# Routed attention with a gated feed-forward: another order of the first microseconds and of the last branch

## The chip, the core and the metric

The kernel runs on one NeuronCore of a Trainium2 chip. A core has five engines, each with its own queue of instructions: TensorE (PE, matrix products; the loading of its stationary operand is shown as PEld), VectorE (DVE), ScalarE (ACT), GpSimd (POOL) and SyncE (SP), which here only issues transfers. Engines wait for each other through semaphores. Products land in PSUM, all else lies in SBUF; transfers between HBM and SBUF go through 16 DMA engines. The metric is the time of one execution on the device in microseconds (us); smaller is better.

## What is computed

The reference has two blocks. The first is attention in which a query sees only keys of its own cluster; the second is a feed-forward with a hard swish. B, H, S, D = 4, 8, 768, 64; there are 16 centroids for each head; the second block has d_model 512 and d_ff 2048. All is float32.

```python
# q, k, v: (4, 8, 768, 64); centroids: (8, 16, 64)
q_assign = argmax(einsum('bhsd,hcd->bhsc', unit(q), unit(centroids)))
k_assign = argmax(einsum('bhsd,hcd->bhsc', unit(k), unit(centroids)))
mask   = q_assign[:, :, :, None] == k_assign[:, :, None, :]
scores = where(mask, (q @ k^T) / 8, -1e9)
attn   = softmax(scores) @ v
x = attn as (4*768, 512)
h = x @ w_in                      # (3072, 2048)
g = h * clip(h + 3, 0, 6) / 6
out = g @ w_out                   # (3072, 512)
```

## The kernel before

**Two paths.** `fast_path` computes the result on the assumption that the data are well-behaved (no ties between clusters, weights in a usual range, no row that sees almost nothing) and keeps sums from which this is read off at the end. It leaves one flag, `ok`. The kernel then loads `ok` into a register of each engine and, under `tc.If(... == 0)` in line 992, runs `general_path`, which computes everything again without the assumption. With the inputs of the reference `ok` is 1 and the general path is skipped, but its instructions stand in the program of each engine all the same: on SyncE 260 of them lie between the branch and what follows the `If`.

**Tiling.** The 32 heads are worked off as 16 pairs (two heads of 64 columns fill the 128 rows of TensorE). For a pair, `load` (line 175) brings q and k in four transfers and v in two. `turn` (line 287) transposes q and k by TensorE, three 128x128 blocks at a time into a PSUM tile `pqk`, and ScalarE copies each tile to `xf`: parts 0 and 1 are q, parts 2 and 3 are k. `cluster_scores` (line 303) multiplies `xf` by the unit centroids `cnT` into `pcs`, and ScalarE copies it to `cs`. `route` (line 314) transposes that back (`pr`), VectorE takes the maximum and writes `one_hot`. `route_turn` (line 343) multiplies `one_hot` by `ident_q` or `ident_k` (the identity, and the identity times -2^60, both bf16) into `po`, and ScalarE copies it to `xm`. Scores are then two products into one PSUM tile `ps`: `scores_qk` (line 361) from `xf`, which needs no routing, and a masked product from `xm`, which adds a huge negative number wherever the clusters differ. ScalarE takes the exponential, GpSimd adds up the rows for the sums, TensorE multiplies by v.

**The loop and what lies beside it.** One loop of 196 half-steps goes over all pairs (12 score tiles each). Beside the scores it works off the next pair's preparation, the decoding of the weights (they arrive as 64-bit numbers) and the products of the feed-forward of the batch before. The order of all engines' instructions is the order in which the program writes them: the whole of this stands under `tc.manual_schedule()`, and no planner moves anything. An engine works its own queue strictly in this order, so an instruction that waits holds up all that stand behind it.

**The prologue** (lines 588 to 603) is what the loop needs for its first pair. In order: the centroids are requested on ScalarE's queue, q and k of pair 0 on SyncE's, then `constants` (line 256: the identity, its two bf16 copies on VectorE, `parity`, and five fills on GpSimd), v and the first piece of the weights, `centroid_norm` (line 271: a chain of small VectorE operations that makes the centroids' rows unit length, spreads them to the two halves, transposes them by TensorE into `pc` and copies that to `cnT`), the four turns, the request for pair 1, two tiles of score products, the cluster scores, the routing. Small PSUM tiles of the prologue (`pqk`, `pc`, `pcs`, `pr`, `po`) come from `psum_m`, which has two buffers; a third tile waits until the first is read. `psum_t`, with one buffer, is used by the decoding of weights. There is one `qk` tile, so pair 1 can be requested only when pair 0 has been turned.

**The end.** After the last product of the feed-forward VectorE reduces the sums to `ok` (lines 646 to 665), each engine loads it, compares, and branches. After the `If` the kernel ends in two barriers over all engines. In the empty arm of the `If` each engine waits for its own semaphores (SyncE for eight).

Of the kernel before, what the change touches and what calls it, by code (L numbers as in the profile page):

```python
# [8 lines left out]
F32 = mybir.dt.float32  # L9
# [9 lines left out]
P = 128  # L19
# [21 lines left out]
FAR = 2.0**60  # L41
# [75 lines left out]
def fast_path(ctx, tc, ok, q, k, v, centroids, moe_w_in, moe_w_out, out):  # L117
# [3 lines left out]
    nc = tc.nc  # L121
# [21 lines left out]
    psum_t = pool("psum_t", 1, space=PSUM)  # L143
# [5 lines left out]
    ident = const.tile([P, P], F32, name="ident")  # L149
    ident_q = const.tile([P, P], BF16, name="ident_q")  # L150
    ident_k = const.tile([P, P], BF16, name="ident_k")
# [12 lines left out]
    st = {}  # L164
    later = []

    def scratch(shape, name):

        if st["early"]:
            return psum_m.tile(shape, F32, name=name, tag="m")  # L170
        return psum_t.tile(shape, F32, name=name, tag="t")
# [3 lines left out]
    def load(g, *names):  # L175
        if g >= NPAIR:
            return
        b, h = divmod(2 * g, H)
        for name in names:
            if name == "v":  # L180
                dst = st["v", g] = vp.tile([P, NCH, 2, D], F32, name="vt")
            elif name == "q":
                st["qk", g] = qkp.tile([P, 2, NCH, 2, D], F32, name="qk")
            if name != "v":
                dst = st["qk", g][:, "qk".index(name)]
            src = {"q": q, "k": k, "v": v}[name]
            for t in range(2):
                nc.sync.dma_start(dst[:, :, t], src[b, h + t].rearrange("(p j) d -> p j d", p=P))
# [66 lines left out]

    def constants():
        make_identity(nc, ident)
        nc.vector.tensor_copy(out=ident_q, in_=ident)
        nc.vector.tensor_scalar_mul(out=ident_k, in0=ident, scalar1=-FAR)
        for t in range(2):  # L260
            nc.vector.tensor_reduce(
                out=parity[:, t : t + 1],
                in_=ident.rearrange("p (h t c) -> p t h c", t=2, c=C)[:, t], axis=AX.XY, op=ALU.max,
            )
        nc.gpsimd.memset(half_c, 0.5)
        nc.gpsimd.memset(low_c, 1.0 / BOUND)
        nc.gpsimd.memset(ones, 1.0)
        nc.gpsimd.memset(w_low, W_LOW)
        nc.gpsimd.memset(one_hot, 0.0)

    def centroid_norm():
        cn = unit_rows(nc, smallp, cen, D)

        nc.scalar.activation(out=w_totals[:, 0, 0:1], in_=w_low, func=ACT.Exp)

        wide = smallp.tile([P, 2, D], F32, name="cenwide")
        for t in range(2):
            nc.vector.tensor_scalar_mul(out=wide[:, t], in0=cn, scalar1=parity[:, t : t + 1])
        pc = scratch([P, P], "pc")
        nc.tensor.transpose(out=pc, in_=wide, identity=ident)  # L280
        nc.vector.tensor_copy(out=cnT, in_=pc)


# [3 lines left out]
    def turn(g, part):  # L287
        if part == 0:
            st["xf", g] = xp.tile([P, NC2, P], F32, name="xf")
        qk, xf = st["qk", g], st["xf", g]  # L290
        pt = scratch([P, NHC, P], "pqk")
        for i in range(NHC):
            j = part * NHC + i
            nc.tensor.transpose(out=pt[:, i], in_=qk[:, j // NCH, j % NCH], identity=ident)  # L294
        dst = xf[:, part * NHC : (part + 1) * NHC]
        nc.scalar.copy(out=dst, in_=pt)  # L296
        if part == 3:
            st.pop(("qk", g))
# [4 lines left out]
    def cluster_scores(g):  # L303
        c0, xf = (2 * g) % H * C, st["xf", g]
        ps = scratch([P, 512], "pcs")[:, 0 : NC2 // 4 * P]
        for a in range(4):
            nc.tensor.matmul(  # L307
                ps[a * 2 * C : (a + 1) * 2 * C], lhsT=cnT[:, c0 : c0 + 2 * C], rhs=xf[:, a::4],
                start=True, stop=True,
            )  # L310
        cs = st["cs", g] = rtp.tile([P, NC2 // 4, P], F32, name="cs")
        nc.scalar.copy(out=cs, in_=ps)

    def route(g):
        cs = st.pop(("cs", g))
        pr = scratch([P, NC2, 2, C], "pr")
        for i in range(NC2 // 4):
            nc.tensor.transpose(out=pr[:, 4 * i : 4 * i + 4], in_=cs[:, i], identity=ident)
        pr = pr.rearrange("p j t c -> p (j t) c")
        mx = rtp.tile([P, 2 * NC2], F32, name="mx")  # L320
        nc.vector.reduce_max(out=mx, in_=pr, axis=AX.X)
        oh = one_hot.rearrange("p j (t c) -> p j t c", t=2)[:, :, :, 0:C]
        pr = pr.rearrange("p (j t) c -> p j t c", t=2)
        mx = mx.rearrange("p (j t) -> p j t", t=2)
        halves = [slice(0, NCH), slice(NCH, NC2)]
        for sl, op in zip(halves, (ALU.is_ge, ALU.is_lt)):
            nc.vector.tensor_tensor(
                out=oh[:, sl], in0=pr[:, sl],
                in1=mx[:, sl].unsqueeze(3).to_broadcast([P, NCH, 2, C]), op=op,
            )  # L330


        def count():
            for a, sl in enumerate(halves):
                seen = rtp.tile([P, NCH, 2, C], BF16, name="seen")
                nc.scalar.activation(
                    out=seen, in_=oh[:, sl], func=ACT.Copy, scale=1.0 - 2 * a,
                    accum_out=counts[:, a, g : g + 1],
                )

        later.append(count)
# [19 lines left out]
    def scores_qk(n):  # L361
        g, hf, j = where(n)
        st["ps", n] = psum_s.tile([P, 2, 512], F32, name="ps")
        scores_part(n, st["xf", g], True)
# [223 lines left out]
    with tc.manual_schedule():  # L588
        nc.scalar.dma_start(cen, centroids.rearrange("h c d -> (h c) d"))
        load(0, "q", "k")  # L590
        constants()
        load(0, "v")
        load_weights(0)
        centroid_norm()
        for part in range(4):
            turn(0, part)
        load(1, "q", "k")
        scores_qk(0)
        scores_qk(1)
        cluster_scores(0)  # L600
        route(0)
        for part in range(3):
            route_turn(0, part)

        for n in range(0, total + lag_d + 2, 2):
            g, r = divmod(n, per_pair)
            for i in (n, n + 1):
                if i < total:
                    scores(i)
            for i in (n - lag_v, n - lag_v + 1):  # L610
                if 0 <= i < total:
                    attn_v(i)
            m = n - lag_d + 1
            if m >= 0 and m % NCH == NCH - 1:
                later.append(divide(m))
            prep = prep_items(g + 1, r)
            if r == 4 and prep:
                prep.pop()()
            if n == DECODED:
                st["early"] = False  # L620
            if m >= 0 and m % per_batch == per_batch - 1:
                fill += ffn_items(m // per_batch)
            if r == 6:
                load(g + 2, "q", "k")
                load(g + 1, "v")
            want = items_by(n + 2) - done if n < total else len(fill)
            want = min(want, len(fill))
            done += want
            for i in range(max(len(prep), want)):
                if i < want:  # L630
                    fill.pop(0)()
                if i < len(prep):
                    prep[i]()
            for step in decode[: share[r]]:
                step()
            del decode[: share[r]]
            for check in checks:
                check()
            checks, later[:] = later[:], []

        for check in checks:
            check()
# [3 lines left out]
    good = smallp.tile([P, 2, NG], F32, name="good")  # L646
    fit = smallp.tile([P, 2, NW], F32, name="fit")
    alone = smallp.tile([P, 2, NPAIR], F32, name="alone")
    for got, sums, *bounds in (
        (good, totals, BOUND, 0.0), (fit, w_totals, W_HIGH, 0.0), (alone, counts, NC2, -NC2 * (C - 1.0)),  # L650
    ):
        for a, bound in enumerate(bounds):
            nc.vector.tensor_scalar(
                out=got[:, a], in0=sums[:, a], scalar1=bound, scalar2=None, op0=ALU.is_le
# [320 lines left out]
@with_exitstack  # L975
def kernel(
    ctx: ExitStack,
    tc: tile.TileContext,
    q: bass.AP,
    k: bass.AP,  # L980
    v: bass.AP,
    centroids: bass.AP,
    moe_w_in: bass.AP,
    moe_w_out: bass.AP,
    out: bass.AP,
):
    ins = (q, k, v, centroids, moe_w_in, moe_w_out)
    flagp = ctx.enter_context(tc.tile_pool(name="flagp", bufs=1))
    ok = flagp.tile([1, 1], I32, name="ok")
    with ExitStack() as inner:  # L990
        fast_path(inner, tc, ok, *ins, out)
    with tc.If(tc.nc.values_load(ok[0:1, 0:1], min_val=0, max_val=1) == 0):
        with ExitStack() as inner:
            general_path(inner, tc, *ins, out)

# [31 lines left out]
```

## Time and profile before

| what | value |
|---|---|
| median of 4 runs | 1071.58 us (1070.57 to 1073.1) |
| the profiled execution, its time | 1072.8 us |
| its span, first to last instruction | 1071.0 us |
| mean granted clock of TensorE | 0.993 |
| first matmul starts | 6.38 us |
| last matmul group ends, `ok` is written | 1063.6 us, 1064.5 us |
| data moved by DMA | 42.9 MB, mean 40 GB/s |

A profile is one execution as the hardware recorded it. Times are in us from the first instruction. `L294` is line 294 of the kernel before. A row such as `PE pqk L294 x12` in the chain is a piece of the path that ended last: twelve instructions of TensorE from line 294, and the numbers before it are its start and its length on the path. The granted clock is the share of its full clock that TensorE was given. A share of DMA over 1 means that some packets overlapped. Transfers and register instructions are not counted as busy.

### The profile page before, as it was taken

The page shows a single profiled execution, that of the slowest core. Times are in us where ns is not written, and L with a number is a line of the kernel's source. Part 1 is how long each engine was busy: PE and PEld are TensorE (multiplying, and loading weights), DVE is VectorE, ACT ScalarE, POOL GpSimd, SP SyncE. Part 2 cuts the span into 40 slices and gives each one's busy share as a digit, 9 for nine tenths or more (in the row PEclk, how much of TensorE's full clock was granted, in tenths as well). Part 3 has the DMA queues.
Part 4 walks back from the last instruction along what each step waited for, and adds up shares of the span by engine and source line. Part 5 has one row for each costly group of instructions (what it writes and reads, how often), then busy time and mean ns, then how long its engine had stood idle before and what let it go on. Part 6 is the DMA issues. An engine that isn't in the chain of part 4 may idle for free.

```text
span 1071.0 us, 13428 instructions
## 1 busy us (share of the span) xinstructions
PE 1034.4 (97%) x5490; PEld 723.7 (68%) x5490; DVE 460.5 (43%) x658; ACT 392.5 (37%) x796; POOL 305.4 (29%) x171
## 2 busy tenths in 40 slices
PE   6999999999999999999999999999999999999997
PEld 3444454546878857667676766767676688888886
DVE  5799987688241331521342342152145132414141
ACT  5888876674121132342432333233233120201010
POOL 2777755554100023232233222222323200000000
PEclk9999999999999999999999999999999999999999
DMA  5444544330000201002020020200000000000000
GB/s 149 109 123 124 143 124 103 84 104 1 20 1 19 46 1 50 14 1 45 21 46 1 20 45 1 64 1 15 20 1 1 10 11 21 0 20 1 20 1 24
DMA packets 83543, 42.94 MB, mean 40 GB/s; under 512 B 76304, under 2 KB 76304, under 8 KB 83472
## 3 DMA queue, kind: packets, MB, share of 16 engines
q1 hardware_dynamic: 83328, 41.95, 15.0%
q8 instruction: 45, 0.74, 0.3%
q14 instruction: 26, 0.21, 0.1%
q10 hardware_dynamic: 144, 0.03, 0.0%
HBM read 35.68 MB, written 6.29 MB: 39 GB/s over the span
## 4 chain that ended last, share of the span: by engine, by line
PE 90%; ACT 5%; DVE 4%; issue 1%; POOL 0%; ACTq 0%; DVEq 0%; POOLq 0%
PE ph L476 31%; PE Y L494 16%; PE ps L370 14%; PE X L494 11%; PE pv L399 11%; PE pqk L294 2%; DVE g_sb L488 2%; PE pd L420 2%; PE po L350 1%; PE pcs L307 1%; DVE rcp L424 1%; ACT ex L382 1%; ACT xm L354 1%; ACT xf L296 1%; ACT g_sb L443 1%
## 5 line engine op out<-in xcount | busy, mean ns | idle before, releaser
L389 POOL TENSOR_TENSOR acc<-acc,ex 128x768 f32<-128x768 f32 x128 | 244.2, 1908 | 368.6 <-ACT ex L382 363.0
L476 PE MATMUL ph<-xT,w_in_sb 128*128 128x256 f32 x1536 | 343.8, 381 | 0.0
L476 PEld LDWEIGHTS ph<-xT,w_in_sb 128*128 128x128 f32 x1536 | 287.8, 190 | 56.3 <-issue 10.2
L443 ACT ACTIVATE g_sb<-ph,half_c 128x512 f32<-128x512 f32 x96 | 66.0, 687 | 316.0 <-PE ph L476 316.0
L444 DVE SCALAR_TENSOR_TENSOR g_sb<-g_sb,ph 128x512 f32<-128x512 f32 x96 | 66.0, 687 | 254.7 <-ACT g_sb L443 254.7
L382 ACT ACTIVATE ex<-ps 128x768 f32<-128x768 f32 x192 | 148.5, 804 | 66.9 <-PE ps L370 66.7
L370 PE MATMUL ps<-xf 64*128 64x384 f32 x768 | 168.2, 517 | 1.2 <-ACT ex L382 0.8
L399 PE MATMUL pv<-ex,vt 128*64 128x384 f32 x768 | 146.1, 502 | 0.0
L424 DVE RECIPROCAL rcp<-pd 128x384 f32<-128x384 f32 x32 | 81.7, 2553 | 62.9 <-PE pd L420 61.0
L386 POOL TENSOR_TENSOR acc<-ex 128x768 f32<-128x768 f32 x32 | 58.9, 1842 | 174.5 <-ACT ex L382 174.5
L488 DVE TENSOR_TENSOR g_sb<-g_sb 128x256 f32<-128x256 f32 x192 | 103.8, 582 | 3.3
L399 PEld LDWEIGHTS pv<-ex,vt 128*64 128x64 f32 x768 | 46.9, 137 | 81.6 <-issue 77.8
L370 PEld LDWEIGHTS ps<-xf 64*128 64x128 f32 x768 | 64.1, 188 | 46.7 <-issue 32.4
L501 DVE TENSOR_TENSOR y<-y,Y 128x256 f32<-128x256 f32 x48 | 20.2, 420 | 171.4 <-PE Y L494 170.6
L494 PE MATMUL Y<-w_out_sb,g_sb 128*128 128x256 f32 x384 | 88.0, 382 | 0.0
L494 PE MATMUL X<-w_out_sb,g_sb 128*128 128x256 f32 x384 | 87.7, 381 | 0.0
L494 PE MATMUL Y<-T,g_sb 128*128 128x256 f32 x384 | 87.0, 380 | 0.0
L494 PEld LDWEIGHTS Y<-w_out_sb,g_sb 128*128 128x128 f32 x384 | 72.0, 190 | 16.5 <-issue 7.2
L494 PEld LDWEIGHTS X<-w_out_sb,g_sb 128*128 128x128 f32 x384 | 72.1, 190 | 14.2 <-issue 3.0
L494 PEld LDWEIGHTS Y<-T,g_sb 128*128 128x128 f32 x384 | 72.1, 190 | 9.3
L370 PE MATMUL ps<-xm 64*128 64x384 bf16 x384 | 64.1, 328 | 0.0
L296 ACT COPY xf<-pqk 128x384 f32<-128x384 f32 x64 | 30.0, 483 | 52.8 <-PE pqk L294 52.8
(83 smaller groups left out, 642.5 us busy)
## 6 DMA issues: line engine op xcount, KB each, us to landing
raw<-in_moe_w_in_dram SPq DMA_DIRECT2D x16, 512.0 KB, 3.9
raw<-in_moe_w_out_dram SPq DMA_DIRECT2D x16, 512.0 KB, 3.5
qk<-in_q_dram SPq DMA_DIRECT2D x32, 192.0 KB, 4.0
qk<-in_k_dram SPq DMA_DIRECT2D x32, 192.0 KB, 4.5
vt<-in_v_dram SPq DMA_DIRECT2D x32, 192.0 KB, 4.2
out_dram<-y SPq DMA_DIRECT2D x24, 256.0 KB, 2.2
cen<-in_centroids_dram ACTq DMA_DIRECT2D x1, 32.0 KB, 1.8
```

The lines of the kernel that those rows point to most:

```text
L296: nc.scalar.copy(out=dst, in_=pt)
L370: nc.tensor.matmul(st["ps", n][:, t, 0:HALF], lhsT=x[r, NCH + j], rhs=x[r, hf * NHC : (hf + 1) * NHC], start=first, stop=not first,)
L382: nc.scalar.activation(out=ex, in_=sc, func=ACT.Exp, scale=SM_SCALE)
L386: nc.gpsimd.tensor_tensor(out=acc, in0=st["ex", n - 1], in1=ex, op=ALU.add)
L389: nc.gpsimd.tensor_tensor(out=acc, in0=acc, in1=ex, op=ALU.add)
L399: nc.tensor.matmul(pv[t * D : (t + 1) * D], lhsT=vt[:, j, t], rhs=ex[:, t], start=(j == 0), stop=(j == NCH - 1),)
L424: nc.vector.reciprocal(out=rcp, in_=pd)
L443: nc.scalar.activation(out=g, in_=h, func=ACT.Relu, bias=half_c, scale=1.0 / 6.0)
L444: nc.vector.scalar_tensor_tensor(out=g, in0=g, scalar=1.0, in1=h, op0=ALU.min, op1=ALU.mult)
L476: nc.tensor.matmul(ph[:, t * HC : (t + 1) * HC], lhsT=w_in_sb[:, kt, f * P : (f + 1) * P], rhs=xT[:, kt, 2 * m * P : 2 * (m + 1) * P], sta ...
L488: nc.vector.tensor_tensor(out=out_, in0=in0, in1=in1, op=op)
L494: nc.tensor.matmul(bank[:, half * HC : (half + 1) * HC], lhsT=g_sb[:, kind, i], rhs=w[:, i], start=(first and i == 0), stop=(last and i == ...
```

## The change

It has four parts.

1. `constants` ends with fourteen transpositions of the identity on TensorE, into a PSUM tile `warm` of `psum_t` that nobody reads.
2. The two bf16 copies of the identity on VectorE move from `constants` to behind the copy of `cnT`.
3. `centroid_norm` stops before the transposition; the rest is a new function, `centroid_turn`, which is called after the four turns. After the request for pair 1 the order becomes: cluster scores, first tile of score products, routing, second tile of score products.
4. The flag's load is written ahead of the `If`, and the `If` is told which arm is to follow the comparison in the program: the empty one. In the program of each engine the arms change places. Before: comparison, general path, empty arm, end; the comparison jumps to the empty arm. After: comparison, empty arm, a jump to the end, general path, end; the comparison is passed through.

The orders of the instructions on ScalarE, GpSimd and SyncE stay as they were up to the last branch.

```diff
     def constants():
         make_identity(nc, ident)
-        nc.vector.tensor_copy(out=ident_q, in_=ident)
-        nc.vector.tensor_scalar_mul(out=ident_k, in0=ident, scalar1=-FAR)
         for t in range(2):
             nc.vector.tensor_reduce(
...
         nc.gpsimd.memset(one_hot, 0.0)
 
+        warm = psum_t.tile([P, 4, P], F32, name="warm", tag="t")
+        for i in range(14):
+            nc.tensor.transpose(out=warm[:, i % 4], in_=ident, identity=ident)
+
     def centroid_norm():
         cn = unit_rows(nc, smallp, cen, D)
...
         for t in range(2):
             nc.vector.tensor_scalar_mul(out=wide[:, t], in0=cn, scalar1=parity[:, t : t + 1])
+        st["wide"] = wide
+
+    def centroid_turn():
         pc = scratch([P, P], "pc")
-        nc.tensor.transpose(out=pc, in_=wide, identity=ident)
+        nc.tensor.transpose(out=pc, in_=st.pop("wide"), identity=ident)
         nc.vector.tensor_copy(out=cnT, in_=pc)
...
         centroid_norm()
         for part in range(4):
             turn(0, part)
+        centroid_turn()
+        nc.vector.tensor_copy(out=ident_q, in_=ident)
+        nc.vector.tensor_scalar_mul(out=ident_k, in0=ident, scalar1=-FAR)
         load(1, "q", "k")
+        cluster_scores(0)
         scores_qk(0)
+        route(0)
         scores_qk(1)
-        cluster_scores(0)
-        route(0)
         for part in range(3):
             route_turn(0, part)
...
-    with tc.If(tc.nc.values_load(ok[0:1, 0:1], min_val=0, max_val=1) == 0):
+    good = tc.nc.values_load(ok[0:1, 0:1], min_val=0, max_val=1)
+    with tc.If(good == 0, preferred_fallthrough_block=False):
         with ExitStack() as inner:
             general_path(inner, tc, *ins, out)
```

## The prediction

> **What bounds the kernel now.** I read the page first (busy shares, the chain), then the chain in order of time from 0 to 20 us, then a table of stretches of TensorE's clock, and last the instructions of line L992, the final branch. From the page:
>
> ```profile
> span 1071.0 us, 13428 instructions
> PE 1034.4 (97%) x5490; PEld 723.7 (68%) x5490; DVE 460.5 (43%) x658; ACT 392.5 (37%) x796; POOL 305.4 (29%) x171
> PE 90%; ACT 5%; DVE 4%; issue 1%; POOL 0%; ACTq 0%; DVEq 0%; POOLq 0%
> ```
>
> TensorE is busy 97% of the span and 90% of the chain. Once the attention loop runs, TensorE's own queue sets the time. So whatever brings the loop's first matmul forward, or takes time from the end, is worth its full length; the change touches only these two ends.
>
> The start, from the chain in order of time (start, length, what):
>
> ```profile
> 5.82 0.43 DVE cenwide L278 x2
> 6.38 0.45 PE pc L280
> 6.83 2.76 PE pqk L294 x12
> 9.59 2.62 PE ps L370 x8
> 12.21 0.83 PE pcs L307 x8
> 13.06 0.49 ACT cs L312
> 13.59 0.56 PE pr L318 x3
> 14.17 0.57 DVE mx L321
> 14.84 0.37 DVE one_hot L327
> 15.26 0.62 PE po L350 x4
> 15.90 0.59 ACT xm L354
> 16.54 0.59 PE po L350 x4
> 17.12 0.75 PE ps L370 x4
> ```
>
> TensorE stands idle until the centroids are ready (6.38). Then everything is one serial string: the score products (2.62) come before the cluster scores, though the routing (13.06 to 15.26) needs only the latter, and TensorE idles while it runs. The loop proper begins with the masked product at 17.12.
>
> The clock, from the table of stretches; the columns are length, TensorE's busy time and count, granted clock, share of the DMA engines, GB/s:
>
> ```profile
> 5.01:8.42 3.41, 2.04 (x9) 1.00 1.21 263
> 15.25:18.66 3.41, 3.15 (x20) 0.50 0.21 85
> 383.89:387.30 3.41, 1.49 (x13) 1.00 0.00 0
> 711.56:714.97 3.41, 2.17 (x11) 1.00 0.00 0
> ```
>
> The granted clock changes in steps of 3.41 us: it was 0.50 from 15.25 to 18.66, and again for one step from 387.30. Both follow a step with gaps: 1.70 us busy before the first, 1.49 before the second; 2.17 (64%) at 711.56 did not bring it down. Clock records begin only at 11.84, so the 1.00 of the first row is no reading. Durations say half speed there: single score products of L370 take 841 ns until 11.6 and 482 ns at 19.4.
>
> The end, instructions of L992 (min/median/max ns, first and last start):
>
> ```profile
> L992 SPq COMPARE_BRANCH  x1: 45/45/45, 1066.0 to 1066.0; - x1
> L992 SPq EVENT_SEMAPHORE  x8: 17/17/17, 1069.1 to 1069.6; - x8
> L992 PEldq COMPARE_BRANCH  x1: 4364/4364/4364, 1065.5 to 1065.5; - x1
> ```
>
> All engines jump over the general path. SP's next instruction comes 3.0 us after its branch, TensorE's 4.4. In between (1066.3 to 1067.0) the instruction queues fetch 8 KB, for TensorE 16 KB.
>
> **The change, part by part.** The sum is made against the profiled execution: 1072.8 us, span 1071.0 and 1.8 around it. The median of the runs is 1071.58, 1.2 lower.
>
> *Fourteen idle transpositions.* They need only `ident` (ready at 1.31). At 2.76/12 = 0.23 each they take 3.2, to 4.6. The trace's landings put the second q transfer at 5.1 and the second k transfer at 6.9, so they lie beside the wait for q and cost nothing; they would cost if q landed before 4.6. What they can give is the clock. The trace speaks against it: the 60% busy step 5.01 to 8.42 held nothing but transpositions, and the products at 9.59 still ran at half speed, while 64% of ordinary matmuls at 711.56 kept the clock. 60% might also lie under the threshold, so I take 0 and keep the gain of the first rival as the other end. The Trainium skill, "TensorE: Matmul & The Clock Gate", Part 4 (PE-mode transpose), states that transposes do not count as TensorE activity for the clock gate; by it these fourteen are worth nothing, and by the same page's Part 1, where 3.4 us of sustained work lifts the clock, they would make the first rival true.
>
> *Two casts moved on VectorE.* `ident_q` held VectorE 1.56 (1.34 to 2.90) while POOL's fill of `one_hot` ran (1.43 to 2.81). `parity` now stands there and may be held as long: `cenwide` is ready between 4.7 and 6.25. Either is before TensorE asks for it (8.4), so this wins nothing by itself. Behind the copy of cnT the casts cost 0.07 to 1.56 each, from 9.15; VectorE's next work is the maximum after 12.4, so 3.1 is covered; beyond that they would delay the routing one for one.
>
> *Queries and keys turned before the centroids.* q: 5.2 + 6 x 0.23 = 6.6, hidden in the wait for k. k: 7.0 + 1.38 = 8.4, and the last copy (0.48) ends at 8.9. The three tiles reuse two PSUM buffers; the copy that frees pc's buffer ends at about 8.4. pc 0.45 to 8.85, cnT's copy 0.29 to 9.15. Before, the last turn ended at 9.59.
>
> *Cluster scores first.* pcs starts at 9.2. Its only row (0.83) is at full clock; twice that is 1.66; I take 1.5, since nothing but transpositions ran before it: 10.7. Then TensorE runs scores_qk(0), half of 2.62, to about 11.9 (the clock should rise at 11.8, as the step 8.42 to 11.84 is now some 76% busy with matmuls). The copy of cs (to 11.2) lies beside it. pr stands behind scores_qk(0) in TensorE's queue, so it starts at 11.9 and not 11.2; +0.56 = 12.5. Maximum and one_hot take as before 1.11 (14.15 to 15.26): po at 13.6. scores_qk(1) (0.75 to 1.31) now fills that gap. **po comes 1.7 us earlier.**
>
> *The half-clock step.* The step 11.84 to 15.25 now holds pr, scores_qk(1), po and the first masked product: 0.5 + 0.75 + 0.65 + 0.4 = 2.3, 67%, over the 64% that kept the clock. If it is kept, po to the first masked product takes 1.4 as for the second pair (34.74 to 36.13) and not 1.86: 0.46. And 17.12 to 18.66, 1.54 at half clock, is done in 0.77. **1.2 us**, between 1.2 and a loss of 0.4 (the third rival).
>
> *Queues.* SP's load of pair 1 (four transfers) waits for the last k transposition, so it goes out at 8.5 instead of 9.62; behind it stands only a weight chunk. Before, its q landed 4.4 after the first issue: at 12.9, needed after 15.3. ACT's and POOL's orders do not change.
>
> *The last branch.* In the built program the empty arm now follows the comparison, but ends in an unconditional jump over the general path. So SP's eight semaphore waits (0.6) come before the jump and the fetch (3.0) after them; the order changes, the sum does not. I take 0. Bounds: -3.0 if the jump is fetched ahead of time, +4.2 if TensorE fetches twice. The Trainium skill, "Runtime: NRT & Kernel Launch", Instruction fetch mechanics, says that a taken branch out of the loaded pages must fetch its target by DMA before going on; by it the new jump pays like the old one.
>
> **Sum:** 1.7 + 1.2 + 0 = 2.9 in the profiled execution: 1069.9. The steps of the clock need not lie the same way in other runs (which spread over 2.5 us), and the median run may hold less of the half clock: 1.7 to 2.9 there. I take 2.6: **1071.6 - 2.6 = 1069.0 us**, own range 1068.3 to 1070.0.
>
> **Rivals.**
> 1. *Transpositions do count.* The step 1.60 to 5.01 is 88% busy and the clock is full from 5.01. Then k is turned at 7.8, pcs starts at 8.55, pr ends at 10.65, po at 11.75, masked product at 13.15: 4.0 + 0.8 = 4.8 gained; or 3.5, if the 56% of the step to 8.42 brings the clock down again. 1066.8 to 1068.1. For it: work of 3.2 us is about a step long. Against: the row 5.01.
> 2. *The jump is fetched ahead.* 3.0 more from the tail: 1066.0. For it: nothing depends on a loaded value any more. Against: 8 KB transfers are seen only after a branch was executed.
> 3. *The half clock moves on.* The step after the prologue falls short, and 3.41 us of dense loop run at half clock, 1.7 lost instead of 0.77: 2.1 - 0.9 = 1.2 gained, 1070.4.
> 4. *Two fetches (slower).* The page behind the comparison is not there and is fetched too, in TensorE's queue at 4.36, less the 0.16 by which TensorE is ahead of SP at the end: +4.2 - 2.6 = +1.6, 1073.2. It decides once a second fetch costs over 2.6. Against: the arm lies next in line.
>
> **Chances:** forecast 0.50; rivals 0.15, 0.13, 0.16, 0.06. The range 1065.6 to 1070.9 leaves out the fourth and the fringes. A measurement tells 0.2% (2.1 us) from no change, so faster means under 1069.4: 0.36 of the forecast, all of the first two, 0.64 in all. Slower over 0.2% is part of the fourth with a worse head: 0.04. The rest is 0.32.
>
> **What would show it.** Right: pc at about 8.4, pcs at 9.2 before any L370, po near 13.6, first masked product near 15.0, no 0.50 between 15 and 19; the fetch of 3.0 still there, after SP's eight waits. Wrong: score products at full speed before 10 (rival 1), no gap behind the jump (rival 2), a first masked product later than 16 (k landed late, or the casts delayed the maximum), or a second gap in the tail.

## The result, and the profile after

| | before | after |
|---|---|---|
| median | 1071.12 us (53 runs) | 1069.04 us (32 runs) |
| lowest to highest | 1069.63 to 1073.43 | 1066.05 to 1071.79 |
| profiled execution, its span | 1072.8, 1071.0 | 1069.8, 1068.0 |

The ratio is 0.998, with a 95% interval of 0.9974 to 0.9986: 2.1 us faster, 1.5 to 2.8. The forecast was 1069.0, 2.6 less than the median known then (1071.58; more runs of before brought it to 1071.12).

The page after, for the two lines shown of before:

```profile
span 1068.0 us, 13462 instructions
PE 89%; ACT 5%; DVE 3%; issue 1%; DMA 0%; SPq 0%; ACTq 0%; DVEq 0%
```

TensorE still carries the chain. The start, from the chain in order of time (start, length, what); line numbers are those of the changed kernel, so L299 is the turn, L312 the cluster scores, L375 the score products, L323 `pr`:

```profile
2.83 4.04 DMA qk<-in_k_dram
6.87 0.14 issue
7.01 1.51 PE pqk L299 x6
8.52 0.42 PE pc L285
8.96 0.30 DVE cnT L286
9.40 1.51 PE pcs L312 x8
10.91 1.58 PE ps L375 x4
12.49 0.83 PE pr L323 x3
13.32 1.07 PE ps L375 x4
14.45 0.41 PE po L355 x4
14.88 1.08 ACT xm L359 x2
16.01 0.50 PE ps L375 x4
```

The chain no longer begins with the centroids but with the landing of k (6.87). Cluster scores start at 9.40 where they started at 12.21, `po` at 14.45 (before 15.26), the first masked product at 16.01 (before 17.12). The prologue is denser but slower: four score products take 1.58 and `pr` 0.83, against 1.31 (half of 2.62) and 0.56 before. The reason stands in the table of stretches (length, TensorE's busy time and count, granted clock, DMA share, GB/s):

```profile
6.93:10.35 3.42, 2.87 (x15) 1.00 0.71 203
10.35:13.76 3.41, 3.41 (x13) 1.00 1.06 237
13.76:17.17 3.41, 2.85 (x26) 1.00 0.40 133
385.81:389.23 3.42, 3.42 (x16) 0.50 0.02 7
645.22:648.63 3.41, 1.76 (x16) 1.00 0.00 0
648.63:652.05 3.42, 3.42 (x22) 1.00 0.02 5
```

Clock records begin at 13.76; the 1.00 of the first two rows is a default and no reading. TensorE had its full clock from 13.76 on, and in the profile of before from 11.84. The step at half clock that followed the prologue of before is gone. Of the two later ones of before (from 387.30 and from 650.13) the first is there again (385.81), the second is not.

The end, the branch's own instructions (min/median/max ns, first and last start):

```profile
L1001 SPq EVENT_SEMAPHORE  x8: 17/17/17, 1063.4 to 1063.9; - x8
L1001 PEldq COMPARE_BRANCH  x2: 83/1926/3770, 1062.2 to 1062.4; - x2
L1001 SPq COMPARE_BRANCH  x2: 43/46/49, 1062.6 to 1063.9; - x2
```

Each engine now has two branches: the comparison, which is passed (TensorE 83 ns), and the jump to the end (TensorE 3.77 us). SyncE passes its comparison at 1062.65, begins its eight waits at 1063.37, jumps at 1063.95, and its next instruction stands at 1066.68.

**Where the time went.** Both profiles can be cut at two points: a fixed masked product of the third pair (the 61st of all masked products in the records; it starts at 80.86 before, 79.18 after), and the writing of `ok` (1064.55 and 1061.20).

| part | before | after | difference |
|---|---|---|---|
| start to the 61st masked product | 80.86 | 79.18 | -1.68 |
| from there to `ok` | 983.69 | 982.02 | -1.67 |
| `ok` to the end | 6.45 | 6.81 | +0.36 |

The middle part is the same work in both kernels. In all twelve profiles of this study it is 980.4 with no half-clock step in it (one profile), 982.0 to 982.1 with one (ten), 983.7 with two (one): each such step costs 1.67, about half of its length of 3.41. Half of the 3.0 us between the two profiled executions is therefore one such step more or less in the loop, not the earlier start.

The first part depends on the steps too. `tail_only` (below) has the prologue of before unchanged, and there the same masked product came at 79.82, 1.04 earlier than in the profile of before: its step after the prologue kept the full clock.

```profile
11.50:14.92 3.42, 1.87 (x15) 1.00 1.04 240
```

With the whole new order it came at 79.18, at 79.21 in `no_warm` and at 77.74 in `no_branch`. So one profile of each kernel cannot say what the new order is worth; the timed runs have to.

### The profile page after: what moved, and what is told of

Its sections match the earlier page's. It is cut to its first block, busy times and chain, and to the rows that moved or that the text cites. A ratio compares the mean times of both kernels' runs of the same rounds, so it can differ in the third digit from the quotient of the medians.

```text
span 1068.0 us, 13462 instructions
## 1 busy us (share of the span) xinstructions
PE 1036.2 (97%) x5504; PEld 727.5 (68%) x5504; DVE 459.3 (43%) x658; ACT 391.9 (37%) x796; POOL 305.3 (29%) x171
## 4 chain that ended last, share of the span: by engine, by line
PE 89%; ACT 5%; DVE 3%; issue 1%; DMA 0%; SPq 0%; ACTq 0%; DVEq 0%
PE ph L481 31%; PE Y L499 16%; PE ps L375 14%; PE X L499 11%; PE pv L404 11%; PE pqk L299 2%; DVE g_sb L493 2%; PE pd L425 2%; PE pcs L312 1%; DVE rcp L429 1%; PE po L355 1%; ACT ex L387 1%; ACT xm L359 1%; ACT xf L301 1%; ACT wsize L214 1%
## 5 line engine op out<-in xcount | busy, mean ns | idle before, releaser
L375 PE MATMUL ps<-xf 64*128 64x384 f32 x768 | 167.5, 514 | 1.2 <-ACT ex L387 0.8
L375 PEld LDWEIGHTS ps<-xf 64*128 64x128 f32 x768 | 63.9, 188 | 47.2 <-issue 33.2
L375 PE MATMUL ps<-xm 64*128 64x384 bf16 x384 | 63.5, 325 | 0.1
```

The lines of the kernel that those rows point to most:

```text
L375: nc.tensor.matmul(st["ps", n][:, t, 0:HALF], lhsT=x[r, NCH + j], rhs=x[r, hf * NHC : (hf + 1) * NHC], start=first, stop=not first,)
```

## The experiments

All were compared with runs of the kernel before on the same chip; a ratio stands with its 95% interval. "First masked product" and "`po`" are starts in the profile of that run.

**Only the branch.**

```diff
 # on the kernel before
-    with tc.If(tc.nc.values_load(ok[0:1, 0:1], min_val=0, max_val=1) == 0):
+    good = tc.nc.values_load(ok[0:1, 0:1], min_val=0, max_val=1)
+    with tc.If(good == 0, preferred_fallthrough_block=False):
```

> The kernel before with the last branch laid out as after, nothing else. My theory: the empty arm's jump pays a fetch like the old branch, and SyncE first pays 0.7 us to pass from the comparison to its eight waits, as the profile after shows (1062.65 to 1063.37). So the stretch from the writing of ok to the end is 6.8 us instead of 6.45, and the time is 1071.4, 0.3 above before. Rival (the layout saves the fetch, and the after profile was an odd one): the stretch is 3.5 to 5 us and the time 1068 to 1070.

Measured: 1070.55 us, 0.9996 (0.9987 to 1.0004): no difference that the runs can tell. The stretch from `ok` to the end is 6.89. The branch's instructions in this run:

```profile
L993 SPq EVENT_SEMAPHORE  x8: 17/17/17, 1064.0 to 1064.5; - x8
L993 PEldq COMPARE_BRANCH  x2: 83/1916/3750, 1062.8 to 1063.0; - x2
L993 SPq COMPARE_BRANCH  x2: 43/46/49, 1063.3 to 1064.6; - x2
```

The picture of the profile after repeats: 0.7 from the comparison to the waits, then the jump and 2.8 until SyncE goes on. The layout does not save the fetch.

**Everything but the branch.** The last edit alone is taken back from the kernel after.

> The kernel after with the last branch laid out as before. My theory: 0.3 better than after, 1068.7; the stretch from the writing of ok to the end is 6.45 us. Rival (the layout saves a fetch): 1 to 3 us worse than after, 1070 to 1072.

Measured: 1069.21 us, 0.9982 (0.9972 to 0.9992), against 0.998 for the whole change. The tail is 6.45. Over all profiles it is 6.42 to 6.64 with the old branch (eight) and 6.67 to 6.89 with the new (four). So the new layout costs about 0.3 us, which the timed runs cannot resolve, and the rival is refuted. This run also showed another position of the clock's steps: full clock began at 10.32 and not at 13.76, and `po` came at 13.02, the first masked product at 14.58. The chain of this run:

```profile
2.83 3.81 DMA qk<-in_k_dram
9.17 1.40 PE pcs L312 x8
10.57 0.84 PE ps L375 x4
11.41 0.50 PE pr L323 x3
13.02 0.41 PE po L355 x4
14.58 0.50 PE ps L375 x4
```

It is the same program up to the last branch, and its first masked product comes 1.4 us earlier. 0.2 of this is k's earlier landing (6.64, after 6.87); the other 1.2 hang on where the steps of the clock fall.

**No idle transpositions.**

```diff
 # on the kernel after
-        warm = psum_t.tile([P, 4, P], F32, name="warm", tag="t")
-        for i in range(14):
-            nc.tensor.transpose(out=warm[:, i % 4], in_=ident, identity=ident)
```

> The kernel after without its fourteen idle transpositions, nothing else. My theory: transpositions do not lift the clock, and these lie in the wait for q, so nothing changes: 1069.0, with the first masked product at 15 to 16.2 as the steps of the clock happen to fall. Rival (the transpositions help by the clock): 1070 or more, and the first full-speed product later than after.

Measured: 1069.75 us, 0.9983 (0.9973 to 0.9992); full clock from 13.87, first masked product at 16.02, as in the profile after. The fourteen change nothing that can be told. This agreed with my theory that transpositions do not count, but does not prove it.

**Ordinary products in their place.**

```diff
 # on the kernel after
-        for i in range(14):
-            nc.tensor.transpose(out=warm[:, i % 4], in_=ident, identity=ident)
+        for i in range(7):
+            nc.tensor.matmul(warm[:, i % 4], lhsT=ident, rhs=ident, start=True, stop=True)
```

> The kernel after with seven ordinary float32 products of the identity (3.0 us at half clock, as long as the fourteen transpositions) in place of the transpositions. My theory: ordinary products count and transpositions do not, so the first record of full clock comes in one of the steps that begin between 2 and 6 us, in about two runs of three; it falls back as only transpositions follow. The q and k transpositions get faster, of which k's are on the path: 0.3 to 0.8 better than after, 1068.2 to 1068.7. Rival (the kind of work does not matter): as after, 1069.0, no record of full clock before 8 us.

Measured: 1069.72 us, 0.9984 (0.9972 to 0.9995), spread from 1065.98 to 1071.57. In the profile, full clock began at 6.37, the first masked product came at 13.99, and the clock did not fall back. Two stretches of this run:

```profile
2.96:6.37 3.41, 2.93 (x15) 1.00 1.04 231
6.37:9.78 3.41, 2.07 (x17) 1.00 0.90 235
```

A step that was 86% busy lifted the clock; one that was 61% busy, two thirds of it with transpositions, kept it. The expected gain did not show in the median. It seemed to favour "products count, transpositions do not", but this step held transpositions too, so kind and density were not yet apart.

**Sixty idle transpositions.** `range(14)` becomes `range(60)`, with the branch as before.

> The order of after, the branch as before, and sixty idle transpositions instead of fourteen, so that they fill more than two whole steps of the clock with nothing else. My theory: transpositions do not lift the clock, so all sixty run at 0.213 us and last 12.8 us, and the first record of full clock begins after the first ordinary products; span about 1074. Rival (they count like products): full clock by 8 us, the sixty last at most 9.8 us.

Measured: one execution, 1071.96 us, its span 1070.0; full clock from 6.20, the sixty last 9.11. The busy time of the two steps, and then the sixty in the timeline (start, length, what):

```profile
2.79:6.20 3.41, 3.41 (x18) 1.00 1.12 236
6.20:9.62 3.42, 3.42 (x33) 1.00 0.92 226
```

```profile
1.36 9.11 PE L271 MATMUL warm<-ident 128*128 128x128 f32 x60 [1.36 <-POOL ident masks.py:199]
```

18 fit into the first step and 33 into the second, with nothing else in either. **My theory fell: transpositions lift the clock like anything else**, if a step is full of them. The steps of all twelve profiles, those of the runs below included, read again with one rule for every kind of work (steps ahead of the first clock record are counted back from it and taken as half clock, as the longer durations there show):

| TensorE's busy share of a step | what the next step had |
|---|---|
| half clock, up to 0.84 (fifteen steps with work; the 0.84 is in the profile after) | half clock |
| half clock, 0.86 (three steps; `no_warm` stayed, `no_branch` and `real_warm` rose) | once half, twice full clock |
| half clock, 0.93 to 1.00 (all such steps, one or more in every profile) | full clock |
| full clock, 0.44 to 0.50 (thirteen steps, in the prologue and the loop) | half clock |
| full clock, 0.51 and more | full clock |
| full clock, 0.43 to 0.45 (the step in which TensorE's work ends, in `clusters_first`, `tail_only` and `long_idle`) | full clock |

So TensorE goes up after a step that was some 86% busy, and within the prologue and the loop it went down after one that was half busy or less. The last row does not fit this lower bound; in `clusters_first` that step is

```profile
1057.80:1061.22 3.42, 1.47 (x8) 1.00 0.21 80
```

and the half clock comes one step later. At the same place steps of 0.40 and less brought the clock down at once, so the lower bound is not a sharp one by this reading, and why is not known.

**Only the turns first.** On the kernel after: no idle work, the branch as before, and

```diff
-        cluster_scores(0)
         scores_qk(0)
-        route(0)
         scores_qk(1)
+        cluster_scores(0)
+        route(0)
```

> Of the new order only the turning of q and k ahead of the centroids (with the moved casts); both tiles of score products stay ahead of the cluster scores, no idle transpositions, the branch as before. My theory: k's landing at 6.9 sets the turns (7.0 to 8.5), score products start at 9.1 instead of 9.5 and run at half clock, so po comes 0.4 to 0.7 earlier than before, at 14.5 to 14.9; time 1070.4. Rival (the turns carry the gain): po at 13.5, 1069.2.

Measured: 1072.14 us, 1.0004 (0.9995 to 1.0013). `po` came at 14.39, a little ahead of the 14.5 to 14.9 expected, and the profiled execution took 1069.5; but the timed runs lie in two groups, 1069.3 to 1070.2 (four) and 1071.9 to 1073.1 (seven). The time expected was missed by 1.7. The granted clock recorded with each run goes with this: it is 0.997 in all four and 0.993 to 0.995 in all seven. A half-clock step of 3.41 us is worth 0.0016 of it, so the slower ones had some one or two such steps more. Where these lay is not shown, as no slower one was profiled; the step with `pr`, from 10.60, was 61% busy in the profile and is a candidate.

**Only the cluster scores first.** On the kernel before:

```diff
+        cluster_scores(0)
         scores_qk(0)
+        route(0)
         scores_qk(1)
-        cluster_scores(0)
-        route(0)
```

> Of the new order only the cluster scores ahead of the score products and the second tile behind the routing; the centroids still come first, all else is as before. My theory: pcs starts at 10.1, when the last copy of the turns ends, at half clock; scores of tile 0 lie beside the copy of cs, tile 1 in the routing's gap; po at 14.0 to 15.3, as the clock's steps fall, 0 to 1.2 earlier than before; time 1070.3. Rival (the order of scores carries the whole gain): po at 13.5, 1069.2.

Measured: 1068.97 us, 0.998 (0.9971 to 0.9989), all runs between 1067.9 and 1069.4. The rival holds: **in the median, this order alone gives as much as the whole change.** The chain of this run (L307 cluster scores, L370 score products, L318 `pr`):

```profile
6.83 2.76 PE pqk L294 x12
9.59 1.41 PE pcs L307 x8
11.00 0.85 PE ps L370 x4
11.85 0.49 PE pr L318 x3
13.45 0.41 PE po L350 x4
15.01 0.50 PE ps L370 x4
```

From 6.38 to 13.2 TensorE has no gap, so the step 6.50 to 9.91 is full, nearly nine tenths of it with transpositions, and the clock is up at 9.91:

```profile
6.50:9.91 3.41, 3.41 (x14) 1.00 0.84 222
```

The kernel after starts its turns earlier, but waits twice for data within these steps (6.69 to 7.01, 8.93 to 9.40). That keeps its step 6.93 to 10.35 at 84%, and in its profile it is overtaken: 16.01 against 15.01.

The equal medians hide two effects. In the profiles, a mean granted clock of 0.996 or 0.997 stood for one half-clock step after the first record, 0.999 for none, 0.993 for three (all have half clock in their last microseconds besides). By the clock recorded with every execution, the profiled ones included (what lies ahead of the first record does not count in it):

| kernel | runs at 0.996 and 0.997, their median | runs at 0.995 or less |
|---|---|---|
| before (in the three sets of experiments) | 31 of 74, 1070.4 us | 43 |
| `turns_first` | 4 of 11, 1069.4 | 7 |
| `clusters_first` | 10 of 11, 1069.0 | 0 |
| after | 18 of 34, 1067.8 | 14 |
| `no_branch`, `no_warm` | 18 of 24, 1068.5 | 6 |
| `real_fill`, `trans_fill`, `best` (below) | 14 of 24, 1067.6 | 3 |

At the same clock the whole change is 2.6 us below before and 1.2 below `clusters_first` (0.5 in `no_branch` and `no_warm`), and `turns_first` is 1.0 below before. So the earlier turns seem to win time, and to lose it again by more runs with further half-clock steps. The gain over before is not only a matter of how many such steps an execution meets, as it stands among runs of like clock.

**Idle work without gaps.** On the kernel after, with the branch as before; `idle(n)` issues n products of the identity into `warm`:

```diff
-        for i in range(14):
-            nc.tensor.transpose(out=warm[:, i % 4], in_=ident, identity=ident)
+        idle(9)       # float32 products of the identity, as above
...
         for part in range(4):
             turn(0, part)
+            if part == 1:
+                idle(2)
         centroid_turn()
+        idle(1)
```

> The order of after, the branch as before, and ordinary float32 products of the identity in place of the idle transpositions: nine at the start, two between q's and k's turns, one behind the centroids' turn. My theory: full clock from a step that begins before 7 us in every run, first masked product at 13.6 to 14.1; time 1068.0, 1.0 below after and 0.8 below the same without idle work. Rival (the idle products themselves delay k's turns, or the clock falls back): first masked product after 14.6, 1069 or more.

Measured: 1067.13 us, 0.9966 (0.9955 to 0.9977), by this ratio 3.6 us below before. Full clock from 5.64, first masked product at 13.66. Its interval overlaps a little with that of the kernel after (0.9974 to 0.9986); the two runs that follow, with ratios of 0.9967 and 0.9966, make it likely that filling the waits is a gain over after as well. By the table above, this lies mostly in fewer runs at 0.995 or less (3 of 24, against 14 of 34).

**The same with transpositions**, 18, 4 and 2 of them:

> As real_fill, but with transpositions of the identity as the idle work, twice as many of them, for each lasts half as long: eighteen at the start, four between q's and k's turns, two behind the centroids' turn. My first theory (transpositions do not count) has fallen with long_idle. New theory: the kind of work does not matter, a step lifts the clock once it is about 86% busy with anything; so full clock begins by 7 us, the first masked product comes at 13.6 to 14.1 and the time is that of real_fill, 1067 to 1068. Rival (transpositions count for less, and need a step without any gap): as after, no full clock before 8 us, 1069.

Measured: 1067.24 us, 0.9967 (0.9956 to 0.9977); full clock from 6.80, first masked product at 13.86. The step that lifted it, and the one after it:

```profile
3.39:6.80 3.41, 3.41 (x18) 1.00 1.02 226
6.80:10.22 3.42, 2.92 (x25) 1.00 0.93 260
```

The runs tell no difference between products and transpositions. What the fourteen lacked in the profile after was length: they end at 4.6, the q turns begin at 5.17, and the step 3.52 to 6.93 is 76% busy. Eighteen without the six fillers behind them were not tried.

**The centroids turned between q and k.** As with the idle products, but

```diff
             if part == 1:
+                centroid_turn()
                 idle(2)
-        centroid_turn()
         idle(1)
```

> As real_fill, with the centroids turned between q and k, where TensorE waits for k anyway (two idle products behind it, one behind k's turns). Theory: pc and the copy of cnT leave the path, so pcs starts behind the last copy of k's turns, at 8.4 instead of 8.8, and the first masked product comes 0.4 earlier than in real_fill, at 13.2; time 1066.7. Rival (k's second part waits for the copy of cnT through the two PSUM buffers): nothing gained, 1067.1 or more.

Measured: 1067.55 us, 0.9966 (0.9956 to 0.9976). Cluster scores start at 8.21 instead of 8.80 and the first masked product at 13.44 instead of 13.66, half of what was expected; pcs took longer here (1.16 until the score products could begin, against 0.79), as its products now wait for the last copies of the turns. The medians do not tell the two apart.

## Why the prediction was right

The total was right: 1069.0 against 1069.04. Its steps were less right than that, and part of the agreement is luck: 2.6 us were taken off a median of 1071.58 that more runs brought to 1071.12, so 2.1 came.

- **Idle transpositions, 0: value right, reason wrong.** The step that failed is the reading of the row 5.01 to 8.42: 60% of transpositions had not lifted the clock, and I took this for a property of transpositions. The other reading, that 60% is under the threshold, was named and set aside, and it is the true one. The Trainium skill, "TensorE: Matmul & The Clock Gate", Part 4 (PE-mode transpose), which I had weighed against the trace, says that transpositions do not engage the clock; here sixty of them lifted it at 6.20, so for these float32 transpositions the measurement decides against it. The same page's Part 1, by which 3.4 us of sustained work release the clock, agrees with the full steps above.
- **Turns and centroids: right.** k's landing at 6.87 opens the chain, the turns end at 8.5 (8.4 expected), pcs starts at 9.40 (9.2). The casts cost nothing: at their new place `ident_q` takes 0.22, and 1.56 before, where GpSimd was filling `one_hot`.
- **`po` 1.7 earlier: twice what the profiled run shows, 0.8.** pcs took 1.51 (1.5 taken). I let the clock rise at 11.8, by the steps of the one profile before. The steps lie elsewhere in each execution, and in the profiled one it rose at 13.76: score products 1.58 instead of about 1.2, `pr` 0.83 instead of 0.56, `po` at 14.45 and not 13.6. In the run with full clock from 10.32 it came at 13.02, 0.2 of it by k's landing. So the term should have been a range, from 0.8 to about 2.
- **The half-clock step, 1.2: gone, as expected.** The step after the prologue was 83% busy (2.85 of 3.41), where 67% had been worked out, and the clock stayed. But up to the third pair the profiled run gained 1.68 in all, where `po` and this step were to give 2.9: 0.8 by `po` and 0.9 by the step. One of its rows was misread: at 36.13 plain score products start and no masked one, and from `po` to the first masked product it took 1.56 (14.45 to 16.01), not 1.4. And the step was gone in `tail_only` as well, whose prologue is the old one (1.87 of 3.42 busy), so that the profile of before had it was in part the position of its steps.
- **The branch, 0: 0.3 too good.** The fetch stayed, as expected. Not expected was 0.7 between SyncE's comparison and its first wait, where ScalarE passes in 0.1. Part of it is given back by a shorter wait at the jump (2.7 against 3.1, from the branch's start).
- **The sum.** 2.9 were forecast for the profiled execution and 3.0 came, but 1.67 of it is the half-clock step near 650 us, which is not in the sum: in the profile the agreement is luck. For the median 2.6 were forecast and 2.1 came; in it are many positions of the steps.
- **Rivals.** The first had the mechanism right (transpositions count) and its place wrong (in the profile after, the two steps that hold the fourteen are 63% and 76% busy). The second (the fetch is saved) and the fourth (two fetches) are refuted by the tails. The argument against the second was misread, though: 8 KB transfers of instructions run all through the execution (queue 14 has two between 30 and 60 us in the profile of before), not only after a branch. The third did not occur in any profile with this order of the prologue.

## What to carry to other kernels

In a short serial prologue, first look for a result that waits in line behind work it does not need: putting the cluster scores ahead of the score products gave as much as the whole change in the median, and filled the gap of the routing as well. Then look at the gaps by the clock's step: an earlier start that brings waits into a step can cost more clock than it wins time, and idle work paid here where it closed the waits up to the first real instructions, and not where it left a gap before them. And a branch whose usual arm comes next in line gained nothing here, as that arm ends in a jump over the unusual one.

## What the runs showed of the hardware that I had not expected

- Going up and coming down have different thresholds: about 86% busy of a 3.41 us step to rise, about half busy or less to fall (in the prologue and the loop 0.50 fell and 0.51 stayed; at the program's end three steps of 0.43 to 0.45 stayed). Transpositions and products both counted.
- One half-clock step inside dense work costs 1.67 us; whether the gaps near 387 and 650 us meet a step in full decides 0 to 3.3 us of an execution. The runs' recorded clocks agree: in the experiments the runs of before had medians of 1070.3 at 0.997, 1071.3 at 0.995 and 1073.2 at 0.993.
- A jump over the general path costs 2.5 to 3.7 us on four engines and 3.8 to 4.6 on TensorE (from its start to the next instruction, all twelve profiles), whether it is a comparison taken or an unconditional jump. Why SyncE alone needs 0.7 to pass an untaken comparison stayed open. That it fetches the next piece of its program there finds no support in the traces: in their last 8 us the profiles before and after have the same ten transfers of instructions.
